# A seven-tap softmax convolution ahead of a gated feed-forward layer: another way into the first window

## The chip, the cores and the metric

The kernel runs on one core of a Trainium2 chip. The core has five engines that run their own instruction streams and meet at semaphores: TensorE (PE, matmuls; its weight loads are shown apart as PEld), VectorE (DVE), ScalarE (ACT), GpSimd (POOL) and SyncE (SP, which here only issues transfers). SP, ScalarE and GpSimd issue DMAs on queues of their own; 16 DMA engines move the data. SBUF holds 128 partitions, and matmul results go to PSUM.

The metric is device microseconds of one execution, the median of several runs. Before the change it is 772.9 us (three runs, 772.88 to 773.17).

## The reference

```python
def _attn_ref(x, weight):                 # x 8 x 4096 x 192, weight 8 heads x 7 taps
    w = exp(weight - weight.max(-1)); w = w / (w.sum(-1) + 1e-9)
    x_pad = concatenate([zeros((B, 6, D)), x], axis=1)
    # out[b, s, head, :] = sum over k of w[head, k] * x_pad[b, s + k, head, :]   (24 columns a head)

def _moe_ref(x, w_gate, w_val, w_out):    # 32768 tokens, 192 -> 1536 -> 192
    gate = maximum(x @ w_gate, 0.0)
    val = x @ w_val
    return gate * val @ w_out
```

Every token's 192 columns are first mixed with those of the six tokens before it, with seven softmax weights for each head of 24 columns. The result goes through a gated layer with 1536 hidden columns. Input and output are fp32; the kernel works in fp16 with fp32 sums.

## The kernel before

The eight batches are taken as four pairs (`b` and `b + 4`, called `st` 0 and 1 in the code). A unit is 1024 tokens of such a pair, so there are 16 units; a window is 512 of these tokens, two to a unit. The convolved x of a unit lies transposed in `xc[u]`: 64 columns of `st` 0 on partitions 0 to 63, the same 64 columns of `st` 1 on 64 to 127, three chunks `c` of 64 columns side by side.

For each window `gate_val` runs 12 groups `f` of 128 hidden columns: six matmuls with `Wg` and six with `Wv` (line 434), each pair of them using one half of the array for one batch; ScalarE applies the relu from PSUM (443), VectorE multiplies by the other PSUM tile into `hT` (444). `project` (447) then multiplies `hT` by `Wo`, ScalarE copies the result out of PSUM and SP stores it. A PSUM tile is two banks; one pool of four such tiles, handed out in turn, serves everything, so an instruction that fills a tile waits for whoever reads the tile of four places earlier.

The convolution is made in three ways.

- Units 2 to 15 are convolved by VectorE, ScalarE and GpSimd alone (`lane_load`, `lane_turn`, `lane_first`, `lane_rest`, `product`, `add`), with the weights in `tap`, one fp32 number per partition, chunk and tap. `lane_turn` transposes with nine DMA transposes on SP's queue.
- Unit 0 is convolved by TensorE against a band matrix: 118 rows (112 tokens and six ahead) by 112 tokens, one band for each head. `conv_dense(g, c)` (249) uses pieces of x as the weights and the band as the moving operand, so the result comes out transposed as `xc` wants it: 40 small matmuls (line 270) and one copy out of PSUM (280) for each chunk. It is called for window 0 (`g` 0) before the first gate group, and for window 1 (`g` 1) ahead of groups 6, 7 and 8 of window 0.
- Unit 1 is convolved the other way round in `conv(g)` (282) for `g` 2 and 3: the band is the weight and x is the moving operand, eight matmuls (292) give token-major results, five ScalarE copies (305) bring them to fp16 `y` in order of columns, and five DMA transposes on SP (324) put them into `xc[1]`.

How the kernel starts matters most here. The schedule is manual: each engine runs its instructions in the order of the program text.

- GpSimd issues the loads of x (`x_h`, with a cast from fp32 to fp16 on the way, lines 92 and 99), makes `eye` (137), issues the loads of `Wg` and `Wv` in five column pieces (`CUTS`, line 157) into partitions 0 to 63, with the second x in between (`load_x(1)`, line 172), and copies the pieces 2, 3 and 4 to partitions 64 to 127 (`pool_halves`, 164). VectorE does these copies for pieces 0 and 1.
- SP and ScalarE each load half of `weight` into `wr`, spread over 64 partitions each (110).
- TensorE runs 17 matmuls on zeros (125), whose result nobody uses.
- The softmax runs on `wr`: VectorE 181 and 182, the Exp on ScalarE 185, VectorE 187 to 189.
- The band: `prod` (218) multiplies shifted views of `eye` by the weights, `blk` (226) sums over the taps to a 32-column block, and ten copies (235 on VectorE, 237 on ScalarE) place the block along the diagonal of the zeroed `bands`.
- `load_taps` (195) copies the weights to `late` on GpSimd, and 20 small DMAs on SP (205) bring them to their partitions in `tap`.

Of the kernel before, what the change touches and what calls it, by code (L numbers as in the profile page):

```python
# [15 lines left out]
def kernel(  # L16
# [30 lines left out]
    GSUB = 5  # L47

# [7 lines left out]
    GROUPS = [(0, [WIN * w + SUB * j for j in range(GSUB)]) for w in range(2)]  # L56
# [17 lines left out]
    def load_x(g):  # L74


        bp, toks = GROUPS[g]
        xt = xpool.tile([128, GSUB, 2, D], F16, name="x_h")
        if toks[0] == 0:
            nc.vector.memset(xt[0:32, 0, :, :], 0.0)  # L80
        for st in range(2):
            b = bp + NB * st
            jj = int(toks[0] == 0)
            last = toks[-1] == S - SUB or toks[-1] - toks[-2] != SUB
            n_full = len(toks) - jj - int(last)
            lo = toks[jj] - PAD
            src = bass.AP(
                tensor=x.tensor,
                offset=x.offset + (b * S + lo) * D,
                ap=[[D, 128], [SUB * D, n_full], [1, D]],  # L90
            )
            nc.gpsimd.dma_start(out=xt[:, jj : jj + n_full, st, :], in_=src)  # L92
            if last:
                nc.gpsimd.dma_start(
                    out=xt[0 : SUB + PAD, len(toks) - 1, st, :],
                    in_=x[b, toks[-1] - PAD : toks[-1] + SUB, :],
                )
        for st in range(2 * int(toks[0] == 0)):
            nc.gpsimd.dma_start(
                out=xt[PAD:128, 0, st, :], in_=x[bp + NB * st, 0 : 128 - PAD, :]  # L100
            )
        return xt

    xts = {}
    xts[0] = load_x(0)

    HH = H // 2
    wr = const.tile([128, HH, KW], FP)
    for half, eng in ((0, nc.sync), (1, nc.scalar)):
        eng.dma_start(  # L110
            out=wr[64 * half : 64 * half + 64],
            in_=bass.AP(
                tensor=weight.tensor,
                offset=weight.offset + half * HH * KW,
                ap=[[0, 64], [KW, HH], [1, KW]],
            ),
        )
    ones = const.tile([128, 32 + KW], FP)
    nc.vector.memset(ones[:], 1.0)
# [3 lines left out]
    ps = psum.tile([128, 2, 512], FP, name="ps")  # L123
    for n in range(17):
        nc.tensor.matmul(  # L125
            out=ps[:, n % 2, :], lhsT=zeros[:, 0:128], rhs=zeros[:], start=True, stop=True
        )

    bands = [const.tile([128, HH, SUB], F16, name=f"band{half}") for half in range(2)]
    for half in range(2):  # L130
        nc.vector.memset(bands[half][:], 0.0)

    eye = const.tile([128, 32 + KW], FP)
    for half in range(2):
        nc.gpsimd.affine_select(
            out=eye[64 * half : 64 * half + 64],
            in_=ones[64 * half : 64 * half + 64],
            pattern=[[-1, 32 + KW]],  # L140
            compare_op=ALU.is_equal,
            fill=0.0,
            base=0,
            channel_multiplier=1,
        )
# [6 lines left out]
    CUTS = [0, 128, 384, 768, 1152, DFF]  # L152
# [12 lines left out]

    def pool_halves(s):
# [3 lines left out]
    for s in range(4):  # L170
        load_w(s)
    xts[1] = load_x(1)
    pool_halves(2)
    load_w(4)
    pool_halves(3)

    we = const.tile([128, HH, KW], FP)
    ex = const.tile([128, HH, KW + 1], FP)
    nc.vector.memset(ex[:], 1e-9)
    mx = const.tile([128, HH, 1], FP)  # L180
    nc.vector.tensor_reduce(out=mx[:], in_=wr[:], axis=mybir.AxisListType.X, op=ALU.max)
    nc.vector.tensor_tensor(  # L182
        out=we[:], in0=wr[:], in1=mx[:].to_broadcast([128, HH, KW]), op=ALU.subtract
    )
    nc.scalar.activation(ex[:, :, 0:KW], we[:], ACTF.Exp)  # L185
    sm = const.tile([128, HH, 1], FP)
    nc.vector.tensor_reduce(out=sm[:], in_=ex[:], axis=mybir.AxisListType.X, op=ALU.add)  # L187
    nc.vector.reciprocal(sm[:], sm[:])
    nc.vector.tensor_tensor(  # L189
        out=we[:], in0=ex[:, :, 0:KW], in1=sm[:].to_broadcast([128, HH, KW]), op=ALU.mult  # L190
    )

    tap = const.tile([128, NCH, KW], FP)

    def load_taps():
        late = const.tile([128, HH, KW], FP)
        nc.gpsimd.tensor_copy(out=late[:], in_=we[:])
        for c in range(NCH):
            r0 = 0
            while r0 < 64:  # L200
                h = (64 * c + r0) // G
                r1 = min(64, G * (h + 1) - 64 * c)
                for half in range(2):
                    p0 = 64 * (h // HH)
                    nc.sync.dma_start(
                        out=tap[64 * half + r0 : 64 * half + r1, c, :],
                        in_=late[p0 : p0 + r1 - r0, h % HH, :],
                    )
                r0 = r1

    load_taps()
    xts[2] = load_x(2)
    pool_halves(4)

    prod = const.tile([128, HH, 32, KW], FP)
    e0 = eye[:, 0:1]
    w0 = we[:, 0:1, 0:1]
    nc.vector.tensor_tensor(  # L218
        out=prod[:],
        in0=bass.AP(tensor=e0.tensor, offset=e0.offset, ap=[e0.ap[0], [0, HH], [1, 32], [1, KW]]),  # L220
# [329 lines left out]
```

## Time and profile before

| what | us |
|---|---|
| median of three runs | 772.9 |
| the profiled execution, its own time | 772.88 |
| its span, first to last instruction | 771.2 |
| gate and value matmuls, L434, in the chain that ended last | 64% of the span |
| projection matmuls, L454, in the chain | 33% of the span |
| one `hT` product on VectorE, L444 | 1.221, 384 times |
| one relu on ScalarE, L443 | 1.023, 384 times |
| one window: 12 groups | 15.6 (288 matmuls of two windows in 31.19) |
| projection of one unit | 15.95 (192 matmuls) |

A unit takes 31.19 + 15.95 = 47.1 us of TensorE, and the chain repeats these two numbers from unit 1 on without a gap. The granted clock is 1.000 in the page's summary.

How it is read: the page gives busy time by engine and by line, the chain of work that ended last (followed back from the last instruction to whatever released each step), and the groups of instructions with their mean duration and the idle time ahead of them. The trace behind it answers for single stretches: a timeline of each engine, waits, and busy time by window. In the timelines a line gives start, length, engine, source line, what was written from what, the number of instructions merged, and in brackets the idle time before with whatever ended it. `SPq` and `POOL ... DMA` lines are the issuing of transfers, not their landing.

### The profile page before, as it was taken

Reading aid. Unit: us, or ns where it says so; the run is one execution under the profiler, and the core shown is the slowest. Engines: PE = TensorE matmul, PEld = TensorE weight load, DVE = VectorE, ACT = ScalarE, POOL = GpSimd, SP = SyncE. Lnnn points to the kernel's source line nnn. Section 1 sums busy time; section 2 is a strip of 40 time slices with the busy share of each in tenths; the row PEclk is TensorE's granted clock in tenths of the full one; section 3 lists DMA queues with packets and bytes.
Section 4 is the critical chain, followed back from the end, with each engine's and each line's share of the span. In section 5 each row is a group of like instructions: output and inputs, shape, how many; then the busy total and the mean of one; then the engine's idle time right before and its main releaser. Section 6 shows DMA issues by size and latency. Waiting matters only on the chain.

```text
span 771.2 us, 19018 instructions
## 1 busy us (share of the span) xinstructions
PE 765.0 (99%) x7953; PEld 500.1 (65%) x7953; DVE 687.0 (89%) x734; ACT 602.1 (78%) x733; POOL 371.3 (48%) x213
## 2 busy tenths in 40 slices
PE   8999999999999999999999999999999999999998
PEld 4485574856748476484765848557485674846648
DVE  7889999989999899999999999999998999986491
ACT  5797887878778787787878878788787877875572
POOL 9607739084480935709266291753908446090000
PEclk9999999999999999999999999999999999999999
DMA  9957828171361803629054291632817122100102
GB/s 115 133 90 127 90 84 94 58 110 11 90 86 63 110 23 84 72 82 95 31 94 52 84 91 42 102 34 83 93 58 107 15 88 43 63 22 22 62 1 83
DMA packets 132597, 55.63 MB, mean 72 GB/s; under 512 B 98208, under 2 KB 132512, under 8 KB 132512
## 3 DMA queue, kind: packets, MB, share of 16 engines
q1 hardware_dynamic: 90480, 38.35, 23.9%
q0 software_dynamic: 41808, 15.97, 19.1%
q8 instruction: 62, 1.02, 0.6%
q14 instruction: 23, 0.19, 0.1%
q10 hardware_dynamic: 224, 0.11, 0.0%
HBM read 31.94 MB, written 25.17 MB: 74 GB/s over the span
## 4 chain that ended last, share of the span: by engine, by line
PE 98%; DVE 1%; DMA 0%; ACT 0%; issue 0%; DVEq 0%; ACTq 0%
PE ps L434 64%; PE ps L454 33%; PE ps L270 0%; DMA wr<-in_weight_dram 0%; PE ps L292 0%; DVE hT L444 0%; DVE prod L218 0%; DVE blk L226 0%; ACT gr L443 0%; DVE band L235 0%; ACT out_s L465 0%; ACT ex L185 0%; DVE we L182 0%; DVE we L189 0%; DVE sm L187 0%
## 5 line engine op out<-in xcount | busy, mean ns | idle before, releaser
L444 DVE TENSOR_TENSOR hT<-gr,ps 128x1024 f16<-128x1024 f16 x384 | 468.7, 1221 | 61.7 <-ACT gr L443 34.9
L443 ACT ACTIVATE gr<-ps 128x1024 f16<-128x1024 f32 x384 | 392.7, 1023 | 101.2 <-PE ps L434 100.9
L387 POOL TENSOR_TENSOR prods<-prods 128x1344 f32<-128x1344 f32 x70 | 212.3, 3033 | 312.2 <-DVE prods L383 286.6
L434 PE MATMUL ps<-xc,Wv 64*128 64x512 f16 x2304 | 311.8, 376 | 0.2 <-DVE hT L444 0.2
L434 PE MATMUL ps<-xc,Wg 64*128 64x512 f16 x2304 | 312.0, 376 | 0.0
L454 PEld LDWEIGHTS <-hT 128*128 128x128 f16 x3072 | 252.7, 98 | 6.4 <-issue 6.4
L454 PE MATMUL ps<-Wo,hT 128*128 128x192 f16 x3072 | 256.4, 246 | 0.0
L434 PEld LDWEIGHTS <-Wv 64*128 64x128 f16 x2304 | 129.8, 94 | 118.9 <-issue 0.5
L434 PEld LDWEIGHTS <-Wg 64*128 64x128 f16 x2304 | 111.1, 94 | 134.6 <-issue 2.4
L410 DVE SCALAR_TENSOR_TENSOR acc<-x_r,tap,acc 128x576 f32<-128x576 f16 x210 | 154.3, 810 | 1.7 <-ACT acc L398 1.7
L381 ACT ACTIVATE prods<-x_r,tap 128x448 f32<-128x448 f16 x222 | 130.1, 660 | 0.0
L465 ACT COPY out_s<-ps 128x768 f32<-128x768 f32 (+1 forms) x65 | 50.8, 782 | 58.0 <-PE ps L454 44.2
L343 POOL DMA_DIRECT2D x_e<-in_x_dram x56 | 45.1, 817 | 3.5 <-POOL x_p L362 2.4
L362 POOL COPY x_p<-x_e 128x1728 f16<-128x1728 f16 x28 | 44.7, 1624 | 3.6 <-DMA x_e<-in_x_dram 3.6
L387 POOL TENSOR_TENSOR xc<-prods 128x1344 f16<-128x1344 f32 x14 | 42.4, 3029 | 1.1
L410 DVE SCALAR_TENSOR_TENSOR xc<-x_r,tap,acc 128x576 f16<-128x576 f16 x42 | 31.8, 810 | 0.0
L398 ACT ACTIVATE acc<-x_r,tap 128x576 f32<-128x576 f16 x42 | 29.3, 764 | 0.0
L383 DVE TENSOR_SCALAR prods<-x_r,tap 128x448 f32<-128x448 f16 x72 | 27.3, 447 | 0.0
L465 DVE COPY out_s<-ps 128x192 f32<-128x192 f32 x1 | 0.4, 357 | 13.4 <-PE ps L454 13.4
L92 POOL DMA_DIRECT2D x_h<-in_x_dram x8 | 6.7, 843 | 0.8 <-POOLq L534 0.8
L125 PE MATMUL ps<-zeros 128*128 128x512 f16 x17 | 5.3, 484 | 1.5 <-DVE zeros L122 1.5
L270 PEld LDWEIGHTS <-x_h 118*32 118x32 f16 (+3 forms) x240 | 3.0, 93 | 3.2 <-issue 3.2
(40 smaller groups left out, 48.8 us busy)
## 6 DMA issues: line engine op xcount, KB each, us to landing
out_dram<-out_s SPq DMA_DIRECT2D x63, 384.0 KB
x_e<-in_x_dram POOLq DMA_DIRECT2D x34, 192.0 KB, 6.8
x_e<-in_x_dram POOLq DMA_DIRECT2D x22, 240.0 KB, 6.2
x_r<-x_p SPq DMA_TRANSPOSE x126
x_h<-in_x_dram POOLq DMA_DIRECT2D x4, 240.0 KB, 5.0
x_h<-in_x_dram POOLq DMA_DIRECT2D x4, 192.0 KB, 4.3
Wo<-in_moe_w_out_dram POOLq DMA_DIRECT2D x1, 576.0 KB, 9.3
Wg<-in_moe_w_gate_dram POOLq DMA_DIRECT2D x3, 144.0 KB, 4.3
```

Source lines behind the costliest of these rows:

```text
L343: nc.gpsimd.dma_start(out=xe[:, j : j + n, st, :, :].rearrange("p j c r -> p j (c r)"), in_=bass.AP(tensor=x.tensor, offset=x.offset + (b ...
L362: nc.gpsimd.tensor_copy(out=xp[:, :, :, st, :], in_=xe[:, :, st, :, :])
L381: engine.activation(out=out, in_=in_, func=ACTF.Copy, scale=scale)
L383: engine.tensor_scalar(out=out, in0=in_, scalar1=scale, scalar2=None, op0=ALU.mult)
L387: nc.gpsimd.tensor_tensor(out=pr[:, 0] if k < KW - 1 else xc[u][:, :, LDVE:UNIT], in0=pr[:, 0], in1=pr[:, k], op=ALU.add,)
L398: nc.scalar.activation(out=accs[u][:, c, :], in_=shifted(u, c, 0, 0), func=ACTF.Copy, scale=tap[:, c, 0:1],)
L410: nc.vector.scalar_tensor_tensor(out=xc[u][:, c, 0:LDVE] if k == KW - 1 else acc[:, c, :], in0=shifted(u, c, k, 0), scalar=tap[:, c, k : k ...
L434: nc.tensor.matmul(out=pss[i][:, st, :], lhsT=W[64 * st : 64 * st + 64, c, 128 * f : 128 * (f + 1)], rhs=xcb[64 * st : 64 * st + 64, c, WI ...
L443: nc.scalar.activation(out=gr[:], in_=pss[0][:], func=ACTF.Relu)
L444: nc.vector.tensor_tensor(out=h[:, f], in0=gr[:], in1=pss[1][:], op=ALU.mult)
L454: nc.tensor.matmul(out=ps[:, i // 2, D * (i % 2) : D * (i % 2) + D], lhsT=h[:, f, st, 128 * q : 128 * (q + 1)], rhs=Wo[:, f, :], start=(f ...
L465: copy(out=os_[:, 0:a, 0:m], in_=ps[:, 0:a, 0:m])
```

## The change

The diff does four things.

1. **Softmax and band.** `weight` is loaded once, as 8 rows of 7. The Exp takes `wr` and the negated maximum as its bias. The weights are scaled into `w8` (8 x 7 taps x 16 copies). `spaced`, made on GpSimd by a select, holds for each of 112 partitions a one in its tap and column with gaps between; two VectorE reduces over it give `places` and `same`, matrices of zeros and ones. One fp32 matmul spreads the weights to 112 partitions, a VectorE product with `same` gives `diag`, and seven matmuls with shifted views of `places` as weights put the whole band (128 x 8 heads x 112) into PSUM; three copies bring it to `bands`. `tap` comes from three fp32 matmuls with `sel` and one copy, in place of the 20 DMAs.
2. **First x.** SP and ScalarE load it as fp32 into the room of `prods`, in four blocks of 104 + 6 rows and a head for each batch (`DSUB` is 104, `ROWS0` 110); ScalarE casts one batch to fp16 `x_h`, VectorE the other. The 17 matmuls on zeros become five, one and one.
3. **Second block.** Window 1 of unit 0 now goes through `conv` like unit 1, in two parts ahead of groups 3 and 4 of window 0, and so through ScalarE's moves and five transposes on SP's queue, into `xc[0]`. `conv` has a `part` argument and takes one PSUM tile at a time.
4. **Weights.** `CUTS` changes; piece 3 is brought to the upper partitions by two DMAs on SP (`dma_halves`), and GpSimd's copy of piece 4 comes later. `load_x(2)` is issued after the first `lane_load`, and the first `gate_val` stands ahead of the first `lane_turn` in the program.

```diff
-    GROUPS = [(0, [WIN * w + SUB * j for j in range(GSUB)]) for w in range(2)]
+    GROUPS = [(0, [DSUB * j for j in range(GSUB)]), (0, [WIN + SUB * j for j in range(GSUB)])]
...
-    xts[0] = load_x(0)
-    HH = H // 2
-    wr = const.tile([128, HH, KW], FP)
-    for half, eng in ((0, nc.sync), (1, nc.scalar)):
...
+    wr = const.tile([H, KW], FP)
+    nc.sync.dma_start(out=wr[:], in_=weight)
+    room = apool.tile([128, KW, NCH, LPOOL], FP, name="prods")
...
+    for st, eng in ((0, nc.sync), (1, nc.scalar)):
+        eng.dma_start(
+            out=stage(ROWS0, 1, GSUB - 1, st),
+            in_=bass.AP(
+                tensor=x.tensor,
+                offset=x.offset + (NB * st * S + DSUB - PAD) * D,
+                ap=[[D, ROWS0], [DSUB * D, GSUB - 1], [1, D]],
+            ),
+        )
+    for st in range(2):
+        nc.vector.memset(stage(32, 0, 1, st), 0.0)
...
+    spaced = const.tile([SUB, KW, SEG + 2 * GAP], FP)
+    nc.gpsimd.memset(spaced[:], 0.0)
+    nc.gpsimd.affine_select(
+        out=spaced[:, :, GAP : GAP + SEG],
+        in_=ones[0:SUB, 0 : KW * SEG].rearrange("p (k s) -> p k s", k=KW),
...
+    def make_sel():
+        nc.gpsimd.memset(sel[:], 1.0)
+        for sign, base in ((1, 0), (-1, G - 1)):
+            nc.gpsimd.affine_select(
...
+    warm_up(5)
...
-    CUTS = [0, 128, 384, 768, 1152, DFF]
+    CUTS = [0, 128, 384, 640, 1024, DFF]
...
+    def dma_halves(s):
+        both_halves(nc.sync.dma_start, s, Wg)
+        both_halves(nc.sync.dma_start, s, Wv)
...
-    for s in range(4):
-        load_w(s)
+    load_w(0)
+    make_sel()
+    load_w(1)
+    load_w(2)
     xts[1] = load_x(1)
+    load_w(3)
     pool_halves(2)
     load_w(4)
-    pool_halves(3)
+    dma_halves(3)
...
-    nc.vector.tensor_tensor(
-        out=we[:], in0=wr[:], in1=mx[:].to_broadcast([128, HH, KW]), op=ALU.subtract
+    nc.vector.tensor_reduce(
+        out=mx[:], in_=wr[:], axis=mybir.AxisListType.X, op=ALU.max, negate=True
     )
-    nc.scalar.activation(ex[:, :, 0:KW], we[:], ACTF.Exp)
+    nc.scalar.activation(ex[:, 0:KW], wr[:], ACTF.Exp, bias=mx[:])
...
+    nc.tensor.matmul(
+        out=spread[0:SUB, 0, 0:H],
+        lhsT=w8[:].rearrange("h k s -> h (k s)"),
+        rhs=spaced[0:H, 0, GAP : GAP + H],
...
+    warm_up(1)
+    diag = const.tile([SUB, H, SEG], F16)
...
+    for b in range(NSEG):
+        nc.tensor.matmul(
+            out=flat[:, 128 * b : 128 * b + H * SEG],
+            lhsT=places[:, SUB - SEG * (b + 1) : SUB - SEG * (b + 1) + 128],
+            rhs=diag[:].rearrange("p h s -> p (h s)"),
...
+    for c in range(NCH):
+        nc.tensor.matmul(
+            out=spread[:, 1, KW * c : KW * (c + 1)],
+            lhsT=sel[:, c, :, :].rearrange("h t r -> h (t r)"),
+            rhs=w8[:, :, 0],
...
+    warm_up(1)
+    xts[0] = xpool.tile([128, GSUB, 2, D], F16, name="x_h")
+    for st, copy in ((0, nc.scalar.copy), (1, nc.vector.tensor_copy)):
+        copy(out=xts[0][0:ROWS0, :, st, :], in_=stage(ROWS0, 0, GSUB, st))
+    bands = const.tile([128, H, SUB], F16)
+    for h0, h1, copy in (
+        (0, 3, nc.scalar.copy),
+        (3, 6, nc.vector.tensor_copy),
+        (6, 8, nc.scalar.copy),
+    ):
...
+    nc.scalar.copy(out=tap[:].rearrange("p c k -> p (c k)"), in_=spread[:, 1, 0 : NCH * KW])
...
-    def conv(g):
+    def conv(g, part):
...
         for jj, t in enumerate(toks):
+            u, k = t // UNIT, min(SUB, UNIT - t % UNIT)
             nc.sync.dma_start_transpose(
-                out=xc[1][:, :, t - UNIT : t - UNIT + SUB],
-                in_=y[0:SUB, jj].rearrange("p c s r -> p (c s r)"),
+                out=xc[u][:, :, t % UNIT : t % UNIT + k],
+                in_=y[0:k, jj].rearrange("p c s r -> p (c s r)"),
             )
...
-            if u == 0 and w == 0 and f in (6, 7, 8):
-                conv_dense(1, f - 6)
+            if u == 0 and w == 0 and f in (3, 4):
+                conv(1, f - 3)
...
+    pool_halves(4)
     lane_load(2)
+    xts[2] = load_x(2)
```

## The prediction

> **What bounds the kernel now.** I read the page's parts 1 and 4 first, then the chain in order of time, then the timelines of ScalarE, GpSimd (POOL) and SyncE (SP) over the first 60 us. The page:
>
> ```profile
> PE 765.0 (99%) x7953; PEld 500.1 (65%) x7953; DVE 687.0 (89%) x734; ACT 602.1 (78%) x733; POOL 371.3 (48%) x213
> PE 98%; DVE 1%; DMA 0%; ACT 0%; issue 0%; DVEq 0%; ACTq 0%
> ```
>
> TensorE is busy or ends the chain nearly everywhere, so time can only come from where it is not yet at work, or from matmuls removed. The chain in order of time (start, length, what):
>
> ```profile
> 0.83 2.98 DMA wr<-in_weight_dram
> ...
> 4.34 0.23 ACT ex L185
> ...
> 5.33 1.10 DVE prod L218
> 6.43 0.02 issue
> 6.45 1.10 DVE blk L226
> ...
> 8.33 1.61 PE ps L270 x102
> 9.94 1.20 PE ps L434 x10
> ...
> 13.50 4.71 PE ps L434 x42
> 18.21 0.56 PE ps L270 x40
> 18.77 1.40 PE ps L434 x12
> ```
>
> The first useful matmul starts at 8.33: 3.81 us until the 8x7 weights `wr` have landed, then 4.52 us of softmax and band. From 13.50 on TensorE never waits. The second conv block (L270 again) costs three pieces of 0.56 and lengthens the following group from 1.30 to 1.40, so 3 x 0.66 = 1.98 us. The first window of gate groups ends at 27.83 (the last of its pieces in TensorE's timeline begins at 27.18 and the next at 27.83).
>
> From the timelines (start, length, engine, line, what, count):
>
> ```profile
> 1.42 1.28 ACT L185 ACT_TABLE_LOAD   x1 [1.42 <-PEq L534]
> 44.12 2.00 ACT L305 CAST y<-ps 112x480 f16<-112x480 f32 x5 [0.17 <-PE ps L292]
> ```
> ```profile
> 9.63 1.75 POOL L92 DMA_DIRECT2D x_h<-in_x_dram  x2
> ```
> ```profile
> 47.08 7.59 SPq L324 DMA_TRANSPOSE xc<-y  x5
> 54.77 0.53 SPq L466 DMA_DIRECT2D out_dram<-out_s  x1
> 55.41 8.48 SPq L324 DMA_TRANSPOSE xc<-y  x5
> ```
>
> The table load is early and hidden. One token-major conv costs ScalarE 2.00 us of moves and SP 7.59 to 8.48 us of transposes; by the trace's landing records the last of the five lands 8.7 and 9.6 us after the first was issued.
>
> **The change, part by part.** The profiled execution took 772.88 us: span 771.2 and 1.7 around it; the median of the runs is 772.9, so one sum serves both.
>
> *Weights and softmax.* `wr` becomes one DMA of 8 rows of 28 B. ScalarE's copy of before (64 rows) landed between 2.61 (first engine) and 3.16 (last), SP's at 3.81, so the new one is bounded by 2.6 and 3.8; I take 2.9, nearest to the smaller copy, a little late because ScalarE's x transfer is issued beside it. The Exp now reads `wr` itself, and in the built program the wait for it sits on the table load: 1.28 us that were hidden come onto the path. Then 0.03 + 1.28 + 0.23 (Exp, L185), reduce 0.20, reciprocal 0.21, scaling 0.22 (between L189's 0.19 and L383's 0.45), all with gaps: 2.2 us from the landing. Next the placing: the fp32 matmul to PSUM, not in the trace, between 0.21 (one L270 matmul) and 0.63 (the longest warm-up one), take 0.4 with its semaphores; `diag` 128 elements from PSUM, 0.3 (L226 and L218 give 1.1 per 896, L465 0.36 per 192); seven loads and matmuls at 83 ns (L454: 192 in 15.95) and the 0.14 hand-over, 0.75; ScalarE's first band copy of 336 elements 0.45 (L305: 320 in 0.45); hand-over 0.14. Sum 2.2 + 0.4 + 0.3 + 0.75 + 0.45 + 0.14, and some gaps of 0.03, gives 4.35. Removed are `prod`, `blk` and the copies (2.9 us), but the path is 4.35 against 4.52: nearly the whole gain is that `wr` lands 0.9 earlier. Start 2.9 + 4.35 = 7.25.
>
> *The first x* must be there too. 836 KB of fp32 go on SP's and ScalarE's queues from about 2.05, when the first packets of before moved. The nearest row is the fp32 store of 768 B packets, which moved at 320 and 336 GB/s in its best half-microseconds: 2.6 us, so x is there by 4.9. The other bound is that only part of the 16 DMA engines work: in the landing records a 24-row `tap` copy posted on 12 engines and an 8-row one on 8. 110 rows spread alike would be 11 engines: 3.8 us, by 6.1. ScalarE's cast of 960 elements takes 0.95 (L443: 1024 in 1.02) and stands ahead of its band copies, so between 5.9 and 7.05 it is done; the band copy wants to start at 6.65. I take 0.25 us as the part not covered: start 7.5, 0.8 earlier than 8.33. The bounds give 6.95 (`wr` at 2.6) and 8.15 (`wr` at 3.8). Between placing and conv TensorE also runs three fp32 matmuls for `tap` and one warm-up, 0.46 to 0.85 (3 x 0.08 to 3 x 0.21, and 0.22); the band copy and its hand-over, 0.59, and the cast cover them, else up to 0.26 is added. The two reduces over `spaced` (about 0.3 each by L226) run while VectorE waits for ScalarE and TensorE.
> The Trainium skill, "DMA: Bandwidth & Descriptors", section "Why a DMA increments its semaphore by 16 and not by 1", says that the engines used are the largest number up to 16 that divides the outer row counts; 12 for 24 rows agrees. By it the 110-row loads get 11 engines, the start is 7.65, and the sum 0.15 us higher.
>
> *Second block token-major.* Three pieces (1.98) become two of four matmuls; eight took 0.82 and 1.00 us at L292, so 0.41 to 0.50 each and the same 0.1 behind: 1.1. Saves 0.8 to 0.9; I take 0.8. ScalarE gets 2.00 us of moves in groups 3 and 4, where it has 1.30 - 1.02 = 0.28 spare per group, against three casts (0.58, 0.69 on VectorE, 0.58) before. Followed through the four PSUM buffers, group 5 waits 0.2 for group 3's VectorE product and group 6 another 0.1: +0.3 (bounds 0 and 2.00 - 1.10 = 0.9).
>
> *Loads moved.* POOL drops four x issues (2.78) and gains memsets and selects. Memset 64x384 took 0.41, select 39 elements 0.24; with 0.4, 0.4 and 0.3, from about 1.0 on, the first weights go out at 2.2 instead of 4.62. Behind them `sel` costs 0.41 and two selects of 384 elements, between 0.24 and 2.4 each (39 to 384 in proportion); I take 0.9, the slope of POOL's plain copies with some more. The second weights then go out at 5.7 (5.93 before), the second x at 8.2 and 9.1 (9.63 and 10.52). It landed at 15.1 and 16.5; less that lead, and with fewer columns ahead of it, about 13.3. It is wanted when group 2 ends: 13.4. Columns 640 to 1023 are now doubled by two DMAs on SP instead of POOL copies: weights there at 14 to 15, plus 2.3 (an unhindered transpose's issue to landing) gives 16.3 to 17.3; group 5 wants them at 17.3 and 17.9. I charge 0.1; if cover is gone the price is in the third rival. The last columns, doubled on POOL, are wanted at 22 and ready near 20.8. Twenty `tap` copies leave SP's queue (17.41 to 34.1), replaced by matmuls that VectorE's and ScalarE's copies hide.
>
> *Late transposes.* The five on SP start when the moves end, 17.2, and land 8.7 to 9.6 later: 25.9 to 26.8. Window 1 starts at 27.83 - 1.2 = 26.6. Charged nothing, with hardly any margin. Behind them SP holds the x_r transposes, wanted only at 46.
>
> Sum: -0.8 - 0.8 + 0.3 + 0.1 = -1.2, so 772.9 - 1.2 = 771.7.
>
> **The rivals.**
> *All in time.* `wr` at 2.6, x by 5, moves fully covered: -1.3 - 0.9 = -2.2, 770.7. For it: before, ScalarE had spare time around its conv casts and no wait followed. Against: everything must come at the better bound.
> *TensorE slow at the start.* Before, 17 warm-up matmuls ran back to back. Counted in half-microseconds (window, length, TensorE busy and count, other engines, clock, DMA):
>
> ```profile
> 3.00:3.50 0.50, 0.50 (x2) 0.15 (x1) 0.00 (x0) 0.00 (x0) 0.50 (x2) 1.00 1.01 50
> 5.00:5.50 0.50, 0.50 (x4) 0.26 (x3) 0.36 (x3) 0.00 (x0) 0.50 (x2) 1.00 1.51 176
> ```
>
> Their starts are 0.427 apart until 4.49 and 0.216 from 4.75: the full rate came 3.1 us after the first. Now five run (2.2 us), then nothing until the fp32 matmul at about 5. If the rate is still half, by that ratio the placing costs up to 0.7 more and the first conv up to 1.6; a switch some 3 us after the placing begins leaves +1.9 of it: 773.6. Against: two more warm-ups and the placing keep TensorE half busy before the conv.
> The Trainium skill, "TensorE: Matmul & The Clock Gate", section "What's actually happening", says about 3.4 us of sustained work open the clock and an idle window closes it; the 3.1 us agree, and by that rule this rival happens.
> *SP's work caught behind POOL's loads (the other side).* At 34.1 to 38.3 four SP transposes were issued while POOL's x loads ran; they landed at 40.8 to 41.6, 6.7 to 3.3 us after issue instead of 2.4. POOL now issues the next x, `x_h` and Wo from about 20 on, the same time as the transposes for window 1, which nothing needed before. With the extra 4.3 the last lands near 30 instead of 26.4: window 1 starts 3.3 late, 774.9 and slower. It decides from a landing after 27.8, where the whole gain is gone; the doubled columns add to it. Against: POOL's copies must end first, so the first three may be through.
> *The start doesn't move.* `wr` at 3.8, SP's landing of before, or x as late: first conv at 8.2, so -0.1 - 0.8 + 0.4 = -0.5: 772.4. For it: ScalarE's x transfer is issued in the same moment, and before, ScalarE's copy landed ahead of SP's.
>
> **How the numbers follow.** 0.2% (1.55 us) is about what a measurement of this kernel tells from no change: below 771.35 is faster, above 774.45 slower. Forecast 0.46 (its own range 770.6 to 772.6; faster 0.22, same 0.24); all in time 0.18 (faster); slow TensorE 0.09 (same 0.07, slower 0.02); caught transposes 0.19 (slower 0.17, same 0.02); no earlier start 0.08 (same 0.07, faster 0.01). Together faster 0.41, same 0.40, slower 0.19. The range 770.0 to 774.8 leaves out about a tenth on each side.
>
> **What would show it.** First conv matmul at 7.5, the table load beginning at `wr`'s landing; warm-up, placing and conv matmuls at the full rate; two pieces of 0.5 in the first window and waits of TensorE on VectorE's product there near 0.3 in all; window 1 beginning at 26.6 with no DMA wait before it. Wrong if TensorE waits for `xc` transposes or for the doubled columns, if the conv pieces run at half rate, or if the start is behind the x cast.

## The result, and the profile after

The changed kernel takes 794.5 us (median of four runs, 793.56 to 795.83) against 772.9 before: a ratio of 1.028, interval 1.0262 to 1.0298. It is 21.6 us slower; the forecast was 771.7, range 770.0 to 774.8. Its profiled execution took 795.05 us with a span of 793.2, so the span grew by 22.0. Among the experiments below one execution each of e5, e6 and e7 ran far longer than all others, 1150.55, 4281.16 and 4626.78 us, and the ratios leave these three out.

The chain of waits after, in order of time (start, length, what), the pieces up to 70 us:

```profile
7.00 0.62 POOL Wv L190
7.62 3.20 POOL x_h L90
10.81 16.58 DMA x_h<-in_x_dram
27.39 0.14 issue
27.53 1.02 PE ps L370 x4
...
38.02 1.53 SPq L407
39.55 0.04 issue
39.60 6.88 DMA xc<-y
46.48 0.25 issue
46.72 18.64 PE ps L517 x144
65.36 1.00 PE ps L370 x8
```

The reader is to see two transfers where the chain of before had matmuls: the second part of the second x, 16.58 us from the start of its issue at 10.81 to its landing at 27.39, and the last transpose of window 1, 6.88 us from 39.60 to 46.48. Window 1 starts at 46.72; before, its first gate group started here:

```profile
27.83 0.81 PE L434 MATMUL ps<-xc,Wg 64*128 64x512 f16 x6
```

That is 18.9 later, and the window takes 18.64 instead of 15.6, 3.0 more. Together 21.9: all of the loss lies ahead of 65.4 us, and from unit 1 on the rhythm of 31.19 and 15.95 is as before.

TensorE's waits over the first 90 us (who waited for whom: total, times, longest):

```profile
PE ps L370 <- DMA x_h<-in_x_dram: 10.5, 1, 10.5
PE ps L517 <- DMA xc<-y: 3.9, 1, 3.9
...
PE ps L517 <- DVE Wg L197: 1.0, 1, 1.0
```

What lies around these waits on TensorE, POOL and VectorE, from the timelines (start, length, engine, line, what, count):

```profile
8.50 3.02 PE L345 MATMUL ps<-bands,x_h 110*32 110x104 f16 x120
```
```profile
7.61 6.36 POOL L90 DMA_DIRECT2D x_h<-in_x_dram  x2
...
29.89 1.47 POOL L197 COPY Wg<-Wg 64x1536 f16<-64x1536 f16 x1 [11.81 <-DMA Wg<-in_moe_w_gate_dram]
...
32.71 3.30 POOL L426 DMA_DIRECT2D x_e<-in_x_dram  x4
```
```profile
9.17 1.67 DVE L197 COPY Wg<-Wg 64x384 f16<-64x384 f16 x1
...
11.72 2.49 DVE L197 COPY Wg<-Wg 64x768 f16<-64x768 f16 x1
```

Three things stand there. The two issues of the second x hold POOL for 6.36 us, where the two of before took 1.75, and every weight piece behind them is late too: POOL waits 11.81 us for the last one. The first conv takes 3.02 us for 120 matmuls, where it took 1.61 for 102. And VectorE's copies of weight pieces of the same sizes take 1.67 and 2.49 us while POOL issues; before, they were:

```profile
8.83 0.29 DVE L164 COPY Wg<-Wg 64x384 f16<-64x384 f16 x1
10.27 0.49 DVE L164 COPY Wg<-Wg 64x768 f16<-64x768 f16 x1
```

Busy time by stretch (window, length, PE, PEld, DVE, ACT, POOL, then the granted clock, DMA share, GB/s), cut where the clock changes:

```profile
11.73:21.97 10.24, 4.28 (x36) 1.56 (x32) 6.47 (x5) 3.50 (x4) 6.31 (x7) 1.00 0.83 65
21.97:32.21 10.24, 4.68 (x22) 2.15 (x24) 0.88 (x1) 2.05 (x3) 2.31 (x2) 0.50 0.54 78
32.21:45.86 13.65, 10.64 (x96) 5.11 (x96) 10.02 (x9) 9.18 (x11) 10.96 (x12) 1.00 1.20 134
45.86:52.69 6.83, 5.97 (x30) 2.47 (x32) 1.78 (x2) 2.05 (x2) 1.40 (x3) 0.50 1.51 186
```

The clock falls to half during each long wait of TensorE and stays there for 4.7 us and 6.0 us after work is back (from 27.53 to 32.21, from 46.72 to 52.69). Work at half rate takes twice as long, so I estimate that each wait costs some 2.3 to 3.0 us more than its own length. Ahead of 11.72 the trace has no record of the clock and the page prints 1.00; that the rate was half there too is read from the matmuls, 3.02 us for the first conv.

### The profile page after: what moved, and what is told of

The parts are those of the page before. It is cut to its first block, busy times and chain, and to the rows that moved or that the text cites. A ratio compares the mean times of both kernels' runs of the same rounds, so it can differ in the third digit from the quotient of the medians.

```text
span 793.2 us, 18787 instructions
## 1 busy us (share of the span) xinstructions
PE 772.1 (97%) x7846; PEld 503.6 (63%) x7846; DVE 688.7 (87%) x728; ACT 604.8 (76%) x736; POOL 373.1 (47%) x210
## 3 DMA queue, kind: packets, MB, share of 16 engines
q0 software_dynamic: 48624, 15.48, 18.9%
## 4 chain that ended last, share of the span: by engine, by line
PE 94%; DMA 3%; POOL 1%; SPq 1%; ACT 0%; issue 0%; DVE 0%; ACTq 0%; POOLq 0%
PE ps L517 62%; PE ps L537 32%; DMA x_h<-in_x_dram 2%; DMA xc<-y 1%; SPq L407 1%; PE ps L370 0%; POOL x_h L90 0%; POOL Wg L190 0%; POOL Wv L190 0%; POOL sel L160 0%; ACT gr L526 0%; POOL sel L158 0%; ACT y L385 0%; POOL spaced L144 0%; ACT out_s L548 0%
## 5 line engine op out<-in xcount | busy, mean ns | idle before, releaser
L517 PE MATMUL ps<-xc,Wg 64*128 64x512 f16 x2304 | 315.3, 379 | 4.9 <-DMA xc<-y 3.9
L385 ACT CAST y<-ps 112x480 f16<-112x480 f32 (+2 forms) x15 | 6.1, 503 | 12.5 <-PE ps L370 12.5
L370 PE MATMUL ps<-x_h,bands 118*112 118x240 f16 x24 | 4.1, 316 | 10.5 <-DMA x_h<-in_x_dram 10.5
L548 DVE COPY out_s<-ps 128x192 f32<-128x192 f32 x1 | 0.4, 357 | 13.4 <-PE ps L537 13.4
L370 PEld LDWEIGHTS <-bands 118*112 118x112 f16 x24 | 3.0, 154 | 12.2 <-issue 12.2
## 6 DMA issues: line engine op xcount, KB each, us to landing
Wo<-in_moe_w_out_dram POOLq DMA_DIRECT2D x1, 576.0 KB, 12.4
x_h<-in_x_dram POOLq DMA_DIRECT2D x2, 221.2 KB, 16.3
```

The costliest lines, as they stand in the source:

```text
L517: nc.tensor.matmul(out=pss[i][:, st, :], lhsT=W[64 * st : 64 * st + 64, c, 128 * f : 128 * (f + 1)], rhs=xcb[64 * st : 64 * st + 64, c, WI ...
L548: copy(out=os_[:, 0:a, 0:m], in_=ps[:, 0:a, 0:m])
```

## The experiments

What the second x has that the x of before had not is its row count. The diff of the section on the change leaves one line out, and it is the one that matters (before, this access pattern, which loads a run of several blocks, had 128 rows each time):

```diff
+        rows = SUB + PAD if g < 2 else 128
...
-                ap=[[D, 128], [SUB * D, n_full], [1, D]],
-            )
-            nc.gpsimd.dma_start(out=xt[:, jj : jj + n_full, st, :], in_=src)
+                ap=[[D, rows], [SUB * D, n_full], [1, D]],
+            )
+            nc.gpsimd.dma_start(out=xt[0:rows, 0:n_full, st, :], in_=src)
```

`SUB + PAD` is 118. My theory was that 118 rows are served by few DMA engines; the rival, that the place of the load in the queues or the clock made the loss.

All runs, with the ratio to the kernel before on the same chip:

| run | edit | median us | ratio, interval |
|---|---|---|---|
| changed kernel | | 794.5 | 1.028 (1.0262 to 1.0298) |
| e1 | 128 rows | 780.2 | 1.0097 (1.0078 to 1.0116) |
| e2 | kernel before, second x 118 rows | 785.8 | 1.017 (1.0154 to 1.0185) |
| e3 | e1, 13 warm-ups | 780.1 | 1.0082 (1.0063 to 1.01) |
| e4 | e1, dense second block | 775.6 | 1.0027 (1.0016 to 1.0038) |
| e5 | e4, 13 warm-ups | 775.4 | 1.0024 (1.0015 to 1.0033) |
| e6 | e3, POOL's loads after the transposes | 777.3 | 1.0045 (1.0031 to 1.0058) |
| e7 | e5, fp32 loads of 112 rows | 775.5 | 1.0024 (1.0015 to 1.0033) |
| e8 | e7, weight pieces as before | 773.3 | 1.0005 (0.9996 to 1.0014) |
| e9 | e8, head loads on two queues | 773.4 | 1.0005 (0.9996 to 1.0013) |
| e10 | token-major again, loads split | 775.9 | 1.0034 (1.0022 to 1.0046) |
| e11 | the same in the changed kernel's load order | 776.7 | 1.0038 (1.0024 to 1.0052) |

### 118 rows: undone, done alone, and measured by itself

e1, the changed kernel with one line edited, and e2, the kernel before with the second x loaded by 118 rows (`rows` in place of 128 for that one load):

```diff
-        rows = SUB + PAD if g < 2 else 128
+        rows = 128
```

> The changed kernel with one edit: the second x is loaded with 128 rows instead of 118. Theory (a load of 118 rows is spread over few of the 16 DMA engines): GpSimd issues each of the two loads in about 0.9 us instead of 3.2, they land 5 to 6 us after issue instead of 16.6, TensorE's wait of 10.5 us for x_h is gone, and with it most of the wait of 3.9 us for the xc transposes and the half-rate stretch behind it; what is left is the first conv at half rate (+1.4) and ScalarE's moves: 772.5 to 775.5. Rival (the second block's way through ScalarE and SP's transposes is the cost, the load is only late behind others): the x wait shrinks by little, 783 to 793.

> The kernel before, with one edit: its second x is loaded with 118 rows instead of 128 (the conv reads 118 in both). Theory of few DMA engines: issue 3.2 us each, landing 16 us after issue, that is at 27 to 29 where the second conv of before wants it at 18.2; the later column pieces, behind it on the same queue, come late too: 781 to 787. Rival (the row count is harmless by itself): 772.5 to 773.5.

e2 came out at 785.8, as the theory said: in the kernel before, 118 rows alone cost 13 us, at an unchanged place in the queues and with the warm-ups of before. Its two loads took 6.32 us to issue and landed at 24.41 and 29.66, and TensorE waited for both:

```profile
24.46 0.23 PE L271 MATMUL ps<-band,x_h 118*32 118x112 f16 x2 [2.79 <-DMA x_h<-in_x_dram]
29.70 1.04 PE L271 MATMUL ps<-band,x_h 118*32 118x112 f16 x38 [5.02 <-DMA x_h<-in_x_dram]
```

e1 came out at 780.2, between the two forecasts. Its second x had landed by 13.88, and the wait for it was gone. 14.3 us are back, and 7.3 of the loss are not the rows. The page's DMA queue lines (packets, MB, share of 16 engines) for the changed kernel and for e1:

```profile
q0 software_dynamic: 48624, 15.48, 18.9%
```
```profile
q0 software_dynamic: 40464, 15.48, 19.0%
```

Fewer rows and 8160 packets more. In the trace the extra packets are of 4 bytes, 350 to 580 in each half-microsecond between 11.5 and 19.5 us, while of the 384-byte packets that carry x only 28 to 63 come in each from 12.5 us on; in e1 they come at 220 to 250 in each between 10.5 and 12.5.

The third kernel measures loads of 5 x 192 numbers at several row counts, on POOL with the cast and on SP as fp32, with VectorE copying 64 x 384 fp16 all the while. It leaves out everything that the reference computes.

> A measurement by itself, none of the reference is computed: GpSimd loads 5 x 192 columns with a cast for 128, 118, 120, 122, 112 and 127 rows, one after the other, while VectorE makes 220 copies of 64 x 384 fp16; then SP loads fp32 for 128, 112, 110 and 118 rows. Theory (the engines used are the largest number up to 16 that divides the rows): 128 and 112 rows use 16 engines and land in 3 to 4 us, 120 uses 15 and lands alike, 118 and 122 use 2 and take 12 us or more, 127 uses 1 and takes 20 or more; on SP 110 takes about 1.4 times as long as 112, 118 five times. VectorE's copies take about 0.3 us except while GpSimd issues the slow ones. Rival (every row count of about 118 is slow, by its size or by the missing rows of the last partitions): 120 as slow as 118, and 112 slow too.

POOL's timeline (issue; the copy behind each waits for its landing) for 128, 118, 120, 122, 112 and 127 rows:

```profile
1.28 1.00 POOL L44 DMA_DIRECT2D pool<-in_x_dram  x1 [0.40 <-issue]
6.88 0.18 POOL L45 COPY seen<-pool 96x1 f16<-96x1 f16 x1 [4.61 <-DMA pool<-in_x_dram]
7.49 3.15 POOL L47 DMA_DIRECT2D pool<-in_x_dram  x1 [0.44 <-issue]
28.31 0.20 POOL L48 COPY seen<-pool 96x1 f16<-96x1 f16 x1 [17.67 <-DMA pool<-in_x_dram]
28.45 0.91 POOL L50 DMA_DIRECT2D pool<-in_x_dram  x1
36.16 0.18 POOL L51 COPY seen<-pool 96x1 f16<-96x1 f16 x1 [6.80 <-DMA pool<-in_x_dram]
36.29 3.23 POOL L53 DMA_DIRECT2D pool<-in_x_dram  x1
51.33 0.18 POOL L54 COPY seen<-pool 96x1 f16<-96x1 f16 x1 [11.81 <-DMA pool<-in_x_dram]
51.45 0.80 POOL L56 DMA_DIRECT2D pool<-in_x_dram  x1
...
55.69 6.15 POOL L59 DMA_DIRECT2D pool<-in_x_dram  x1
84.54 0.18 POOL L60 COPY seen<-pool 96x1 f16<-96x1 f16 x1 [22.70 <-DMA pool<-in_x_dram]
```

From issue to the copy: 5.6 us for 128 rows (with a load on SP beside it, and more than the 3 to 4 expected), 20.8 for 118 (an SP load of 118 rows ran beside it for the last 13), 7.7 for 120 (beside the rest of that load), 15.0 for 122, 3.9 for 112, 28.8 for 127. 112 rows land in a quarter of the time of 122: what counts is the divisor, not the size. 112, 120 and 128 have divisors of 16, 15 and 16; the largest divisor of 118 and of 122 up to 16 is 2, that of 127 is 1. The packets agree: those of 384 bytes came at some 280 to 390 per us with 112, 120 and 128 rows, at 63 with 118 and 122, and at 31 with 127. The issue itself grows the same way, 0.8 to 1.0, 3.2 and 6.15 us. On SP, fp32 loads of 112 rows were read 3.7 us after issue, of 110 rows 4.9, of 118 rows 20.8; the last two ran beside POOL's load of 118 rows, so both figures of 20.8 are too long by what each took from the other.

The Trainium skill, "DMA: Bandwidth & Descriptors", section "Why a DMA increments its semaphore by 16 and not by 1", gives just this rule, the largest count up to 16 that divides the outer dimensions. These loads agree with it, and not with the exception that it names for some copies issued by GpSimd, which by my estimate (8 rows to an engine) would have put 118 rows on 15 engines.

### What was left at 128 rows

In e1 the wait for x was gone, but window 1 still waited for the transposes:

```profile
33.20 1.03 PE L517 MATMUL ps<-xc,Wg 64*128 64x512 f16 x6 [3.15 <-DMA xc<-y]
```

e3 warms TensorE up longer, to price the half clock at the start:

```diff
-    warm_up(5)
+    warm_up(13)
```

> The changed kernel with 128 rows for the second x and 13 matmuls on zeros at the start instead of 5. Theory (the first conv ran at half rate because TensorE was not kept busy in the 3 us before it): the first conv takes about 1.6 us instead of 3.0 and the first gate groups run at full rate; 1.2 to 1.8 us below the run with 128 rows alone. Rival (the half rate doesn't cost, since the loads of weights are wanted later anyway): within 0.4 us of it.

The first conv ran at full rate (1.54 us), window 0 was done about 1.6 us sooner, and the time stayed at 780.1, as its rival said. In the traced executions the wait for the transposes grew by 2.4 and took it all; the runs of each kernel lie up to 4 us apart, so the medians alone could not exclude a gain of a microsecond. TensorE's timeline in e3 at that place:

```profile
34.00 1.47 PE L517 MATMUL ps<-xc,Wg 64*128 64x512 f16 x6 [5.57 <-DMA xc<-y]
```

So something other than TensorE sets when the transposes land. In e3 they were issued from 18.92 on, and POOL's x_e, x_h and Wo loads from 19.67 to 25.70. e4 and e5 (with 5 and 13 warm-ups) take the transposes away: the second block goes back to `conv_dense` ahead of groups 6, 7 and 8. e6 leaves them and moves the loads behind them:

```diff
-            if u == 0 and w == 0 and f in (3, 4):
-                conv(1, f - 3)
+            if u == 0 and w == 0 and f in (6, 7, 8):
+                conv_dense(1, f - 6)
...
```
```diff
-    lane_load(2)
-    xts[2] = load_x(2)
-    nc.gpsimd.dma_start(out=Wo[:], in_=moe_w_out.rearrange("(c p) d -> p c d", p=128))
...
             hs.append(gate_val(0, 0))
+            seen = const.tile([128, 1], F16)
+            nc.gpsimd.tensor_copy(out=seen[:], in_=xc[0][:, 0, UNIT - 1 : UNIT])
+            lane_load(2)
+            xts[2] = load_x(2)
+            nc.gpsimd.dma_start(out=Wo[:], in_=moe_w_out.rearrange("(c p) d -> p c d", p=128))
```

> The changed kernel with x loads of 128 rows and, besides, the second block convolved as before (dense, channel-major, 120 matmuls for each third ahead of gate groups 6, 7 and 8, blocks of 112 tokens), so that window 1 is written by ScalarE and VectorE copies and no transpose on SP stands ahead of it. Theory (what is left of the loss at 128 rows is the five transposes landing late behind POOL's loads, and the half clock after that wait): in the kernel with 128 rows alone window 0 was done at 33.20 - 3.15 = 30.05 us; the dense form costs 0.8 more, so window 1 starts about 30.9 instead of 27.83 in the kernel before: 772.9 + 3.0 = 775.9, 775 to 777, and the wait of window 1 is 0. Rival (the token-major form isn't what costs; the weights, the lanes or the clock are): no change against 780.2, 779 to 782.

> As the one before (128 rows, dense second block), with 13 warm-up matmuls instead of 5. Theory: without the transposes' wait a faster window 0 is no longer swallowed: with 13 warm-ups it was done at 34.00 - 5.57 = 28.43; plus 0.8 for the dense form 29.2, so 772.9 + 1.4 = 774.3, 773.3 to 775.3, that is 1.6 less than with 5 warm-ups. Rival (the clock at the start is hidden by something else too): the same as with 5 warm-ups within 0.4.

> The changed kernel with x loads of 128 rows and 13 warm-ups, token-major second block as changed; POOL's later loads (the two x_e parts, x_h of the third block, Wo) are issued only when the last transpose of the first unit has landed (a POOL copy of its last column stands ahead of them). Theory (POOL's loads hold the transposes up): the five transposes take about 3 us from issue to landing instead of 8.2, the wait of window 1 goes from 5.57 to under 1.5, and window 1 starts about 28.5 to 29.5: 773.5 to 775 if nothing later wants the loads sooner. Rival (five transposes on one queue take that long by themselves): the wait stays above 4 us and the time at 779 to 781. A third outcome: the wait goes but the time comes back later, as a wait for Wo, x_e or x_h: then the trace names it.

e4 came as the theory said, 775.6; e5 gained nothing on it, as its rival said. e6 gives the direct answer, in SP's and POOL's timelines:

```profile
18.80 6.64 SPq L407 DMA_TRANSPOSE xc<-y  x5
```
```profile
26.70 0.19 POOL L576 COPY seen<-xc 128x1 f16<-128x1 f16 x1 [6.72 <-DMA xc<-y]
27.17 3.30 POOL L426 DMA_DIRECT2D x_e<-in_x_dram  x4 [0.27 <-issue]
```

With no POOL load beside them, five transposes issued from 18.80 had landed by 26.70, 7.9 us; in e3, beside the loads, the last landed some 14.8 us after the first issue. Most of the 7.9 is the issue of five, 6.64 us by itself: the last one landed 2.4 us after its own issue (24.19 to 26.58; 3 were expected), where in e3 it took 8.2 (25.57 to 33.76). TensorE did not wait for them, and both windows were done at 43.77 (43.46 before). The time was still 777.3, the third outcome: x_e, issued 7.5 us later than in e3, made the lanes of the third unit late, and the chain runs through their `x_r` transposes and VectorE's `acc` until 67.90. The three loads cannot simply go behind. e6 moves all three at once and does not tell which of them holds the transposes up.

### The start, and the version that comes out even

e5 should have gained 1.6 us over e4 and gained nothing. e7 fetches the first x by 112 rows, which 16 divides, instead of 110:

```diff
-            out=stage(ROWS0, 1, GSUB - 1, st),
+            out=stage(SUB, 1, GSUB - 1, st),
...
-                ap=[[D, ROWS0], [DSUB * D, GSUB - 1], [1, D]],
+                ap=[[D, SUB], [DSUB * D, GSUB - 1], [1, D]],
```

> As the kernel with 128 rows, dense second block and 13 warm-ups, with the two fp32 loads of the first x fetching 112 rows instead of 110 (the two extra rows are read by nothing that counts). Theory (110 rows go to 11 engines, 112 to 16: in the row-count measurement 110 rows were read 4.85 us after issue, 112 rows 3.6): x is cast 0.5 to 1.2 us sooner and the time is 0.5 to 1.2 below the same kernel with 110 rows. Rival (the short head loads or the queue's order set the landing): no difference, within 0.3.

No gain in time, as its rival said, but TensorE's timeline says why:

```profile
7.91 1.54 PE L346 MATMUL ps<-bands,x_h 110*32 110x104 f16 x120
...
18.50 0.82 PE L518 MATMUL ps<-xc,Wg 64*128 64x512 f16 x5 [1.89 <-DMA Wg<-Wg]
```

VectorE's cast of x began at 6.58, where the changed kernel had 7.57, and the first conv at 7.91. In e5 that was 9.33, but there the warm-ups held TensorE until 7.01 and here until 5.68, so the difference between the two starts is the clock's, not the rows'. Then group 5 waited 1.89 us for the columns that SP doubles (0.61 in e5). An earlier start met a fixed landing at 18.5. e8 brings back the weight pieces of before (cuts, order, doubling on POOL), and e9 also puts the second short head load on ScalarE's queue and zeroes the head rows first:

```diff
-    CUTS = [0, 128, 384, 640, 1024, DFF]
+    CUTS = [0, 128, 384, 768, 1152, DFF]
...
     load_w(2)
+    load_w(3)
     xts[1] = load_x(1)
-    load_w(3)
     pool_halves(2)
     load_w(4)
-    dma_halves(3)
+    pool_halves(3)
```

> As the kernel with 128 rows, dense second block, 13 warm-ups and fp32 loads of 112 rows, with the weight pieces cut, ordered and doubled as in the kernel before (cuts at 768 and 1152, the fourth piece loaded ahead of the second x, third and fourth piece doubled by POOL, nothing doubled by SP). Theory (the only thing that swallowed the earlier start there was TensorE's wait of 1.89 us for the columns that SP doubles): no wait in window 0, first conv at about 7.9, both windows done at 45.26 - 1.89 = 43.4 or a little earlier, so 773.7 - 1.9 + the 1.8 between span and time = 773.6 at most and 772.4 if the 0.42 us of the earlier start are kept: 771.8 to 773.6. Rival (the granted clock decides when the first conv is fast, and it rises at another moment in each execution): 773.5 to 775.

> As the one before it in this list, with VectorE's two zeroings of the staged head rows ahead of its other memsets and the second short head load on ScalarE's queue instead of SP's. Theory (the second head load, issued at 2.1 us on SP, is the last part of the first x): VectorE's cast starts 0.3 to 0.6 us sooner and the time falls by as much. Rival (the large fp32 loads land last): no difference, within 0.2.

e8 is at 773.3, within its forecast and even with the kernel before. Its runs form two groups, six at 772.7 to 773.3 and five at 774.3 (the traced one is of these), so the rival, that the moment of the full clock decides, is not ruled out. e9 changes nothing against e8: its cast waited for `diag`, and `diag` for the warm-ups, which end at 6.7 when the clock is late. In the seven executions with 13 warm-ups whose trace shows the moment, the full rate came at 4.19, 5.21, 5.55, 5.78, 6.23, 7.16 and 7.24 us; e7's start at 7.91 and e8's at 8.92 differ as the ends of their warm-ups do, 5.68 and 6.69. The Trainium skill, "TensorE: Matmul & The Clock Gate", section "What's actually happening", says that the window in which activity is counted runs freely and does not start with the kernel; the spread of 3.0 us agrees. So the new way to the band gives a start between 7.9 and 9.4, around the 8.33 of before.

e10 and e11 try to keep the token-major form: x_e is issued ahead of the last pair of POOL copies, x_h and Wo behind the transposes, e10 with the weight pieces of before, e11 with the second x ahead of the fourth piece and SP doubling it:

```diff
+    lane_load(2)
     pool_halves(4)
-    lane_load(2)
-    xts[2] = load_x(2)
...
+            xts[2] = load_x(2)
```

> Token-major second block as in the changed kernel, x loads of 128 rows, fp32 loads of 112 rows, 13 warm-ups, weight pieces as in the kernel before, heads on two queues; POOL loads x_e right behind the fourth doubled piece (ahead of the last one), and x_h of the third block and Wo only when the last transpose of the first unit has landed. Theory (it is the traffic of POOL's loads at the time of the transposes that holds them): x_e moves from about 14.5 to 24 us, the last transpose lands by 27 to 28.5 and window 1 waits under 1 us; the lanes of the third unit aren't late since x_e is early: 771.2 to 773. Rival (x_e's traffic alone is enough to hold the transposes): window 1 waits 2 to 5 us and the time is 774.5 to 778.

> Token-major second block and load order of the changed kernel (second x ahead of the fourth weight piece, which SP doubles), with x loads of 128 rows, fp32 loads of 112 rows, heads on two queues, 13 warm-ups, weight cuts at 768 and 1152, x_e loaded ahead of the doubling of the last piece, and x_h of the third block and Wo only when the last transpose of the first unit has landed. Theory (in the kernel with loads after the transposes both windows took 33.06 us from the end of the first conv, against 33.59 in the kernel before, and nothing but the late x_e came back later; in the kernel with split loads only the second x, 1.9 us late behind the fourth piece, came back): no wait in window 0 or 1 above 0.5 us, both windows done at 42.6 to 43.7, time 771.9 to 773.3 by the moment the granted clock rises. Rival (x_e's traffic holds the transposes, or SP's doubled columns come late again): a wait of 1.5 to 4 us ahead of gate group 6 or of window 1, 774 to 777.

Both missed. In e10 nothing waited for `xc`, as expected, though the last transpose landed 8.9 us after the first issue; x_e alone was in flight beside them. But the second x, now behind the fourth piece, was late:

```profile
16.56 0.59 PE L370 MATMUL ps<-x_h,bands 118*112 118x240 f16 x4 [1.90 <-DMA x_h<-in_x_dram]
```

In e11 it was 1.89 us late again, now behind a third piece of 384 columns instead of 256, and SP's doubled columns, beside x_e, cost two waits more; `Wv`'s took 8.82 us from issue to landing. The traced execution of e11 is its slowest, 780.88:

```profile
24.00 0.82 PE L517 MATMUL ps<-xc,Wg 64*128 64x512 f16 x5 [1.75 <-DMA Wg<-Wg]
...
26.42 1.46 PE L517 MATMUL ps<-xc,Wv 64*128 64x512 f16 x5 [1.59 <-DMA Wv<-Wv]
```

In these two, what was pulled out of the crowd between 8 and 28 us pushed another transfer into TensorE's way. No version here beats the kernel before.

## Why the prediction was wrong, point by point

**The second x: the step that failed.** The prediction put it as "the second x at 8.2 and 9.1", landing "about 13.3", wanted at 13.4. It was issued at 7.61, as early as hoped, and landed at 27.39. The step moved the landing of before (15.1, 16.5) by the lead, as though the transfer were the same. It had 118 rows instead of 128, and the step put that at nothing. The reasoning by the lead was sound: with 128 rows the second x landed at 13.88 (e1), 13.59 (e3) and 13.60 (e4). The prediction cites the rule on row counts and applies it to the 110 rows of the first x, not to the 118 of the second. Price, by e2, e1 and the changed kernel: 13.0 to 14.3 us, three fifths to two thirds of the loss, with its followers (POOL's issue of 3.2 us instead of 0.87, the weight pieces behind it, VectorE's copies, the clock after the wait).

**Late transposes: the rival that happened.** "Charged nothing, with hardly any margin" was wrong; the third rival named the mechanism, POOL's x_e, x_h and Wo beside the transposes, with 4.3 us. The landing that was forecast without that traffic, 25.9 to 26.8, is what e6 showed (by 26.70), in part by luck: the first was issued at 18.80 instead of 17.2 and the five took 7.9 us instead of 8.7 to 9.6. Beside it the last one landed 4.5 us (e1, 12.4 after the first issue against 7.9) to 6.9 us (e3) later. Price: e1 against e4, 4.6 us by the medians and 5.4 by the ratios, of which the wait is 3.15 and the half clock after it, which the prediction did not charge, 1.8 (window 1 took 17.40 instead of 15.6). One outcome does not show that the chance of 0.19 was too low, but the reason for it was weak: two streams that were known to collide were set to the same time. Its sum has a slip too: 26.4 and 4.3 are 30.7, so window 1 would start 4.1 late and the time be 775.8, not 774.9; both lie outside the range given.

**The clock at the start: also happened.** The second rival charged 1.9 us. The first conv took 3.02 instead of 1.61, and full rate came at 11.72 (4.58 before). e4, whose other losses are small, is 2.1 us (0.27%) above the kernel before, of which the first conv is 1.4 and the first gate groups some 0.65: the price was right. Two warm-ups and the placing did not open the clock. The three prices account for the loss: 14.3, 4.6 to 5.4 and 2.1 make 21.0 to 21.8 of the 21.6 us.

**The start.** `wr` landed at 2.2, earlier than the 2.9 taken, and the table load stood behind it as forecast. The x did not follow: ScalarE's cast began at 7.12, a microsecond after the bound of 6.1 for 11 engines. With 112 rows both casts began 0.8 to 1.0 us sooner (e7, 6.36 and 6.58; 7.12 and 7.57 in the changed kernel), so the row count is most of that. But TensorE was not free either: its placing ended at 6.49, and the three `tap` matmuls with the warm-up, taken at 0.46 to 0.85, took some 1.9 us at the half rate, until 8.41, when the bands were ready too (8.44). So the first conv came at 8.50, not 7.5, from two causes that met. In the working, 2.05 and a transfer of 2.6 or 3.8 give 4.65 or 5.85, where it has x by 4.9 or 6.1; the quarter of a microsecond between has no row.

**The doubled columns.** Forecast for 16.3 to 17.3 and charged 0.1; at 128 rows TensorE could use them from 18.5 on (e5, e7), and they cost 0.6 to 1.9 once the rest was in time.

**Right, but worth little.** The token-major form does spare matmuls: in e6 both windows took 33.06 us from the end of the first conv against 33.59 before, so 0.5, which is what the sum had (0.8 less 0.3). The moves on ScalarE and POOL's memsets (0.28 to 0.41) were near the forecast; a select of 384 elements took 0.55 instead of 0.9.

## What to carry to other kernels

Price a transfer by its shape, not by the bytes it shares with its predecessor: loading ten rows fewer here cost 13 us, because the largest divisor of 118 up to 16 is 2. The block needs 118 rows; 128 were right (e1), and by the row-count measurement 120 would have done, though no run of the kernel has them. Where a change makes a transfer newly urgent, ask what else is issued in the same stretch. And when an early gain vanishes, look for the next fixed landing behind it: twice a faster start only met a longer wait.

## What the runs showed of the hardware

**A slow issue on POOL holds VectorE's copies up.** In the row-count measurement VectorE copied 64 x 384 fp16 without a pause. By stretch (window, length, VectorE's busy time and count, clock, DMA share, GB/s):

```profile
7.50:10.60 3.10, 3.05 (x2) 1.00 0.41 131
12.00:18.00 6.00, 5.28 (x22) 1.00 0.86 83
36.30:39.50 3.20, 3.14 (x2) 1.00 0.00 0
41.00:47.00 6.00, 5.28 (x22) 1.00 0.45 25
55.70:61.80 6.10, 6.03 (x3) 1.00 0.00 0
```

One copy takes 0.24 us in the quiet stretches and 1.5 to 2.0 while POOL issues 118, 122 or 127 rows (first, third and last line). With 120 rows three copies fitted into the 0.91 us of the issue. So the long issue costs the neighbour too, which fits the 1.67 and 2.49 us of the changed kernel; in e1, with short issues, the same two copies took 0.29 and 0.82, and e2's long ones brought a copy of 2.79. A long issue is not the only thing that slows them: in e8 two copies of 768 columns took 1.33 and 1.23 us beside POOL's own copies. What in the issue holds VectorE up is not shown.

**The half clock outlasts the wait.** After a wait of 10.5 us TensorE worked for 4.7 us at half rate, after one of 3.9 for 6.0; in e3, after 5.57, for 4.0, and in e1, after 3.15, for 3.4. A single wait of 1.89 or 1.90 us (e7, e10) dropped no clock, while e11's 1.75 and 1.59 close together did, from 26.26 on. By these runs a wait of 3 us or more in a dense stretch is estimated at 1.7 to 3.0 us on top of its length, half of the time at half rate.
